# State updates of a retention layer in column tiles, one chunk's v on another DMA queue, and three chunks' attention one tile later

## The chip, the cores and the metric

The kernel runs on one core of one Trainium2 chip. The metric is the device time of one execution in microseconds (us); lower is better. Five executions of the kernel before gave 211.85 to 213.12 us, with a median of 212.31 us. One of these executions (212.75 us) was taken with the hardware profiler, and all views of the kernel before are of that one.

## What is computed

The first half is a retention layer (linear attention with a decay for each head), the second a two-layer network with a gelu between its layers, without biases. Cut to what matters:

```python
batch, n_heads, seq, head_dim = (4, 8, 768, 64)     # q, k, v
gamma = 1.0 - 2.0 ** (-5.0 - np.arange(H))
for t in range(S):
    state = gamma * state + einsum('bhd,bhe->bhde', k[:, :, t], v[:, :, t])
    y[:, :, t] = (1 / sqrt(D)) * einsum('bhd,bhde->bhe', q[:, :, t], state)
x = y.transpose(0, 2, 1, 3).reshape(B * S, H * D)   # 3072 tokens of 512
h = x @ w_in                                        # 512 x 2048
out = gelu_tanh(h) @ w_out                          # 2048 x 512
```

All inputs and the output are float32 in HBM; the kernel computes its matmuls in float16 with float32 sums.

## The kernel before

**Chunks.** The 768 steps of the sequence are cut into 6 chunks of 128 (c = 0 to 5). One chunk holds 128 steps of all 4 batches, 512 tokens. A chunk goes through attention first (all 8 heads, handled as 4 pairs, `hp` for the pair and `j` for the head in it) and then through the network. While the network of one chunk runs on TensorE, the attention of the next is mixed in.

**Attention of a chunk and batch.** k and q are scaled by powers of the decay. A is k times q transposed (`mm_A`), and is masked on VectorE (`ev_A`, tile a_sb). y is the sum of the old state times q (`mm_yc`, tile st, not in chunk 0) and of v times A (`mm_yi`); `ev_Y` casts it into xT, on ScalarE or VectorE. S is k times v, summed over the steps of the chunk; `ev_S` or `ev_S2` adds it to the decayed state stg and writes st; `decay` (GpSimd) makes the next stg from st. S has two forms in the kernel before. In chunks 0 and 1, `mm_s` multiplies a pair of heads at once, 4 matmuls of 128 columns for a batch, of which `ev_S` reads the two diagonal blocks. In chunks 2 to 4, `att_S2` makes one matmul of 64 columns for each head, 8 for a batch, in column tiles (two heads of a pair write the two halves of the PSUM partitions), the same tiling in which `mm_yi` makes y. Chunk 5 needs no S.

**Transposes.** For chunks 0 and 1, q and k are transposed on TensorE (`mm_T`, `mm_T1`). From chunk 2 on, they are loaded a second way, in blocks of 32 (`load_blk`: 16 transfers of 64 KB for q, tile q, and 16 for k, tile kT), scaled by `prep_blk` on GpSimd (L206) and transposed on VectorE (`tr`, L263). k itself is loaded too (`load1`, L98), since S needs it untransposed.

**Network.** `moe1` makes h_ps for one sixteenth of the 2048 columns of w_in (4 matmuls of 512 columns) and `gelu` (ScalarE) writes g. `moe2` makes a quarter of o_ps of one batch (4 matmuls of 512 columns), and `ev_O` copies the finished o_ps to o_sb and issues its store, on GpSimd for most chunks. A unit below is one call of either, in chunks 2 to 5: 16 of `moe1`, then 16 of `moe2`, four for each batch.

**Order.** The order of the work on each engine is the order in which the program writes it; no scheduler moves anything. `run(units, after)` writes the units one after the other, and behind unit i the calls listed in `after[i]`. That is where the attention of the next chunk sits among the matmuls of this one. On its engine each instruction waits for what it needs, and all behind it wait too. PSUM has 8 banks, of which `bank` hands out 2 under the tag h, 2 under o and 4 under att, in turn, so that a tile waits for the one that had its bank before.

**Loads.** SyncE issues most loads, one after another, in program order: the rest of chunk 1, then q and kT blocks of chunk 2, then three outputs of chunk 0 kept back in `late`, then k of chunk 2, then all of chunk 3 (`load(3)`). In the built program each transfer of SyncE or ScalarE also waits for a semaphore last used by the one issued eight earlier. v of chunks 0, 1 and 3 to 5 is loaded as float32 and cast (on ScalarE, VectorE or GpSimd, `prep1`). v of chunk 2 alone comes through `load_v16`: GpSimd issues four transfers that convert to float16 on the way, with no cast behind them. GpSimd's list around it is:

```python
            7: [(prep, 2, "Q"), (load_v16, 2)],
            8: [(tr, 2, "q")],
            10: [(prep, 2, "Kk")],
```

Capital letters in `prep` stand for the block form (`prep_blk`), small ones for `prep1`. The first loads of chunk 1 on SyncE are held back with a dummy copy (`hold`, L124) until the third part of w_out has landed.

Of the kernel before, what the change touches and what calls it, by code (L numbers as in the profile page):

```python
# [16 lines left out]
def kernel(  # L17
# [11 lines left out]
    C = 128  # L29
# [67 lines left out]
    def load1(eng, nm, c, b):  # L97
        eng.dma_start(  # L98
            out=ld_tile(nm, c, b),
            in_=srcs[nm][b, :, c * C:(c + 1) * C, :].rearrange("h p d -> p h d"),  # L100
        )
# [81 lines left out]
    def prep1(eng, nm, c, b):  # L183
        t = pre.tile(
            [128, H, Dh], F16, tag=f"{nm}16", bufs=6 if nm == "q" else 2 * B, name=f"{nm}16"
        )
        src = ld_tile(nm, c, b)
        if nm == "v":
            if eng is nc.scalar:
                eng.copy(out=t, in_=src)  # L190
            else:
                eng.tensor_copy(out=t, in_=src)
        else:
            col = OQ if nm == "q" else OK
            eng.tensor_tensor(  # L195
                out=t,
                in0=src,
                in1=cst[:, col:col + H].unsqueeze(2).broadcast_to([128, H, Dh]),
                op=ALU.mult,
            )  # L200
        h16[nm, c, b] = t
# [12 lines left out]
    def pair(t, hp):  # L214
        return t[:, 2 * hp:2 * hp + 2]
# [6 lines left out]
    def copy_on(eng, out, in_):  # L222
        if eng is nc.scalar:
            eng.copy(out=out, in_=in_)  # L224
        else:
            eng.tensor_copy(out=out, in_=in_)  # L226
# [5 lines left out]
    def bank(tag, dt=F32, shape=(128, NHP, 128), name="ps"):  # L232
        return psum.tile(list(shape), dt, tag=tag, bufs=BANKS[tag], name=name)
# [70 lines left out]
    def mm_yi(c, b):  # L304
        y_ps = pss["Y", c, b]
        for hp in range(NHP):
            for j in range(2):
                nc.tensor.matmul(  # L308
                    out=y_ps[j * 64:(j + 1) * 64, hp],
                    lhsT=h16["v", c, b][:, 2 * hp + j],  # L310
                    rhs=a_sb[c, b, j][:, hp],
                    start=(c == 0),
                    stop=True,
                    skip_group_check=True,
                )

    def ev_Y(c, b, eng=nc.vector):
        if c not in xT:
            xT[c] = xp.tile([128, NHP, B * C], F16, tag="x", name="xT")
        copy_on(eng, xT[c][:, :, b * C:(b + 1) * C], pss.pop(("Y", c, b)))  # L320

    def mm_s(c, b, tag="att"):
        if c + 1 >= NCk:
            return
        s_ps = pss["S", c, b] = bank(tag, name="s_ps")
        for hp in range(NHP):
            nc.tensor.matmul(  # L327
                out=s_ps[:, hp],
                lhsT=pair(h16["k", c, b], hp),
                rhs=pair(h16["v", c, b], hp),  # L330
                start=True,
                stop=True,
            )

    def ev_S(c, b, eng=nc.vector):
        if c + 1 >= NCk:
            return
        s_ps = pss.pop(("S", c, b))
        for j in range(2):
            sl = slice(j * 64, (j + 1) * 64)  # L340
            if c == 0:
                copy_on(eng, st[sl, :, b, sl], s_ps[sl, :, sl])
            else:
                eng.tensor_tensor(  # L344
                    out=st[sl, :, b, sl],
                    in0=s_ps[sl, :, sl],
                    in1=stg[sl, :, b, sl],
                    op=ALU.add,
                )

    def decay(c, b):
        if c + 2 < NCk:
            nc.gpsimd.tensor_tensor(  # L353
                out=stg[:, :, b],
                in0=st[:, :, b],
                in1=cst[:, OG:OG + NHP].unsqueeze(2).broadcast_to([128, NHP, 128]),
                op=ALU.mult,
            )
# [3 lines left out]
            mm_T(c, b)  # L362
            ev_T(c, b)

    def att_S2(c):

        if c + 1 >= NCk:
            return
        for b in range(0, B, 2):
            s_ps = bank("att", shape=(128, 2, NHP, 64), name="s_ps")  # L370
            for i in range(2):
                for hp in range(NHP):
                    for j in range(2):
                        nc.tensor.matmul(  # L374
                            out=s_ps[j * 64:(j + 1) * 64, i, hp],
                            lhsT=h16["k", c, b + i][:, 2 * hp + j],
                            rhs=h16["v", c, b + i][:, 2 * hp + j],
                            start=True,
                            stop=True,
                            skip_group_check=True,  # L380
                        )
            pss["S2", c, b] = s_ps

    def ev_S2(c, b):
        if c + 1 >= NCk:
            return
        s_ps = pss["S2", c, b // 2 * 2]
        for j in range(2):
            sl = slice(j * 64, (j + 1) * 64)
            nc.vector.tensor_tensor(  # L390
                out=st[sl, :, b, sl],
                in0=s_ps[sl, b % 2],
                in1=stg[sl, :, b, sl],
                op=ALU.add,
            )
        decay(c, b)

    def att_S(c, b, tag="att"):
        mm_s(c, b, tag)
        ev_S(c, b)  # L400
        decay(c, b)

    def att_Y(c):

        tags = ("h", "h", "att", "att")
        for b in range(B):
            mm_yc(c, b, tags[b])
        for b in range(B):
            mm_yi(c, b)
        att_S2(c)  # L410
        for b in range(B):
            ev_Y(c, b, (AC, VE)[b % 2])

    def att_AY(c, bs, tag, ca, abs_, eng):


        for b in bs:
            mm_yc(c, b, tag)
        for b in abs_:
            mm_A(ca, b)  # L420
        for b in bs:
            mm_yi(c, b)
        if tag == "o":
            for b in abs_:
                ev_A(ca, b)
        for b in bs:
            ev_Y(c, b, eng)
        if tag != "o":
            for b in abs_:
                ev_A(ca, b)  # L430
# [184 lines left out]
    ev_T1("q", 0, 3, AC)  # L615
    spin(4)
    mm_A(0, 3)
    mm_s(0, 0)
    mm_yc(0, 2, "o")
    mm_yi(0, 2)  # L620
    prep1(AC, "v", 0, 3)
    ev_Y(0, 2, AC)
    ev_A(0, 3)
# [3 lines left out]
    m1a = [moe1_parts(0, fp, *t01) for fp in range(2)]  # L627
    m1a[0](range(2))
    m1a[1](range(2))
    mm_s(0, 1)  # L630
    mm_yc(0, 3, "o")
    mm_yi(0, 3)
    ev_Y(0, 3)
    mm_s(0, 2)
    mm_s(0, 3)
    m1a[0](range(2, 4))
    m1a[1](range(2, 4))
    for b in range(2):
        moe1_two(0, b, *t23, "oh"[b])
    for b in range(B):  # L640
        ev_S(0, b)
        decay(0, b)


    hold("q", 1, 1, w_out_sb[2][0:1, 0, 0:1])
# [23 lines left out]
    for nm, b in (  # L669
# [9 lines left out]
            11: [(load1, AC, "v", 1, 2), (prep1, AC, "v", 1, 0), (att_AY, 1, (), "att", 1, (0,), None)],  # L679
            12: [(prep1, AC, "v", 1, 1), (att_T, 1, 1), (preps, 1, 2)],  # L680
            13: [(att_AY, 1, (0,), "h", 1, (1,), AC)],
            14: [(prep1, AC, "v", 1, 2), (att_T, 1, 2), (preps, 1, 3), (att_S, 1, 0)],
            15: [
                (att_AY, 1, (1,), "h", 1, (2,), AC),
                (att_T, 1, 3),
                (att_S, 1, 1),
            ],
        },
    )
# [3 lines left out]
    load_blk("k", 2)  # L693
    for rows, o_sb in late:
        nc.sync.dma_start(out=rows, in_=o_sb)
    for b in range(B):
        load1(SY, "k", 2, b)
    load(3)

    def load_v16(c):  # L700

        for b in range(B):
            t = pre.tile([128, H, Dh], F16, tag="v16", bufs=2 * B, name="v16")
            nc.gpsimd.dma_start(
                out=t, in_=v[b, :, c * C:(c + 1) * C, :].rearrange("h p d -> p h d")
            )
            h16["v", c, b] = t

    def prep(c, nms):

        for nm in nms:
# [9 lines left out]
        {  # L721
            0: [(prep1, AC, "v", 1, 3)],
            1: [(att_AY, 1, (2,), "o", 1, (3,), VE)],
            3: [(att_S, 1, 2)],
            4: [(att_AY, 1, (3,), "o", 1, (), VE)],
            6: [(att_S, 1, 3)],
            7: [(prep, 2, "Q"), (load_v16, 2)],
            8: [(tr, 2, "q")],
            10: [(prep, 2, "Kk")],
        },  # L730
    )
    run(
# [2 lines left out]
            1: [(tr, 2, "k", 0, 1)],  # L735
            3: [(att_AY, 2, (), "att", 2, (0, 1), None), (tr, 2, "k", 2, 3)],
            7: [(att_AY, 2, (), "att", 2, (2, 3), None)],
            11: [(att_Y, 2)],
            12: [(ev_S2, 2, 0)],
            13: [(ev_S2, 2, 1)],  # L740
            14: [(ev_S2, 2, 2)],
            15: [(ev_S2, 2, 3)],
        },
    )

# [1 line left out]
    for c in range(2, NCk - 1):  # L747
        n = c + 1
        after = {
            2: [(prep, n, "QKvk"), (tr, n, "q")],  # L750
            9: [(load, n + 1)] if n + 1 < NCk else [],
            15: [(tr, n, "k", 0, 1)],
            18: [(att_AY, n, (), "att", n, (0, 1), None), (tr, n, "k", 2, 3)],
            22: [(att_AY, n, (), "att", n, (2, 3), None)],
            26: [(att_Y, n)],
            27: [(ev_S2, n, 0)],
            28: [(ev_S2, n, 1)],
            29: [(ev_S2, n, 2)],
            30: [(ev_S2, n, 3)],
        }  # L760
        run(
            [(lambda fc=fc: moe1(c, fc)) for fc in range(NF)]
            + [x for b in range(B) for x in units2(c, b)],
            after,
        )
# [37 lines left out]
```

## Time and profile before

| | value |
|---|---|
| median of 5 executions | 212.31 us (211.85 to 213.12) |
| the profiled execution | 212.75 us, span 210.7 us (first to last instruction) |
| granted TensorE clock | full, in all 40 slices |
| busy: TensorE, GpSimd, VectorE, ScalarE | 203.9, 102.0, 92.3, 83.6 us |
| o_ps matmuls of 512 columns (L513) | 368, one each 0.216 us when back to back |
| h_ps matmuls of 512 columns (L468) | 304, likewise |
| SyncE's queue (q1) | 20.22 MB, 50.1% of 16 engines' span |
| GpSimd's queue (q0) | 9.44 MB, 21.9% |

A line of the timeline gives the start and the length of a group of like instructions in us, the engine, the source line, the output and inputs, the shape and the count, and in brackets how long the engine had been idle before it and which instruction ended that. PE is TensorE's matmul stream, DVE VectorE, ACT ScalarE, POOL GpSimd, SPq the DMA issues of SyncE. The chain of work is followed back from the last instruction to what released it, step by step; a line gives start, length and what it was. The 0.216 us above is 13.81 us of the chain for 64 h_ps matmuls.

### The profile page before, as it was taken

The numbers are of one execution on the slowest core, as the hardware profiler recorded it, in microseconds if no ns is written. First come the engines' busy times: TensorE is split into PE (matmuls) and PEld (weight loads), VectorE is DVE, ScalarE is ACT, GpSimd is POOL, SyncE is SP. The second block draws the span as 40 slices with busy tenths as digits, with TensorE's granted clock in tenths as the row PEclk, the third lists the DMA queues.
The fourth block names the chain that finished last, engine by engine and source line by source line (L and its number), as shares of the span: only waits on it lengthen the run. The fifth ranks groups of instructions, "written<-read, shape, count | busy, mean of one in ns | idle before, by whom it ended". The sixth has DMA issues, their size and how long they took to land.

```text
span 210.7 us, 3948 instructions
## 1 busy us (share of the span) xinstructions
PE 203.9 (97%) x1550; PEld 109.5 (52%) x1550; DVE 92.3 (44%) x163; ACT 83.6 (40%) x142; POOL 102.0 (48%) x123
## 2 busy tenths in 40 slices
PE   7999999999999699999999999999999999999993
PEld 2458444467886246444446444456444455444452
DVE  5797100399542675450767352567460552100001
ACT  2375660246464113366113466113466113565120
POOL 3589300317278756862892959731598411100100
PEclk9999999999999999999999999999999999999999
DMA  7999999998879997979979899897996021100112
GB/s 160 288 237 169 206 202 199 272 237 171 130 110 125 241 188 183 215 121 186 270 123 200 174 203 238 158 199 121 206 252 136 0 101 53 50 0 0 53 54 97
DMA packets 132691, 33.32 MB, mean 158 GB/s; under 512 B 126528, under 2 KB 130880, under 8 KB 132672
## 3 DMA queue, kind: packets, MB, share of 16 engines
q1 hardware_dynamic: 111088, 20.22, 50.1%
q0 software_dynamic: 9856, 9.44, 21.9%
q10 hardware_dynamic: 11728, 3.41, 7.1%
q8 instruction: 12, 0.20, 0.4%
q14 instruction: 7, 0.06, 0.1%
HBM read 31.48 MB, written 6.29 MB: 179 GB/s over the span
## 4 chain that ended last, share of the span: by engine, by line
PE 83%; SPq 8%; DVE 3%; DMA 2%; issue 2%; POOL 1%; DVEq 0%
PE o_ps L513 37%; PE h_ps L468 33%; SPq L110 8%; PE spin_ps L171 3%; PE a_ps L273 2%; PE y_ps L308 2%; DMA kT<-in_k_dram 2%; PE y_ps L295 2%; DVE q L195 1%; POOL kT L206 1%; PE s_ps L374 1%; DVE a_sb L286 1%; PE qkT_ps L239 1%; PE qkT_ps L252 1%; PE s_ps L327 1%
## 5 line engine op out<-in xcount | busy, mean ns | idle before, releaser
L513 PE MATMUL o_ps<-w_out,g 128*128 128x512 f16 (+1 forms) x400 | 86.9, 371 | 0.0
L468 PE MATMUL h_ps<-xT,w_in 128*128 128x512 f16 (+1 forms) x464 | 85.1, 342 | 0.0
L483 ACT ACTIVATE g<-h_ps 128x512 f16<-128x512 f32 x96 | 56.9, 597 | 44.8 <-PE h_ps L468 44.7
L468 PEld LDWEIGHTS <-w_in 128*128 128x128 f16 x464 | 45.0, 98 | 37.7 <-issue 0.3
L513 PEld LDWEIGHTS <-g 128*128 128x128 f16 x400 | 37.9, 98 | 41.1 <-issue 0.2
L286 DVE TENSOR_TENSOR a_sb<-a_ps,mask 128x512 f16<-128x512 f32 x48 | 30.1, 682 | 17.2 <-PE a_ps L273 17.0
L535 ACT COPY o_sb<-o_ps 128x512 f32<-128x512 f32 x19 | 11.1, 586 | 53.8 <-PE o_ps L513 51.0
L195 POOL TENSOR_TENSOR k<-k,cst 128x512 f16<-128x512 f32 x23 | 23.9, 1061 | 16.1 <-DMA k<-in_k_dram 16.1
L540 POOL DMA_DIRECT2D out_dram<-o_sb x18 | 10.1, 562 | 44.6 <-ACT o_sb L535 34.7
L206 POOL TENSOR_TENSOR kT<-kT,cst 128x512 f16<-128x512 f32 x16 | 16.2, 1042 | 8.8 <-DMA kT<-in_k_dram 6.5
L353 POOL TENSOR_TENSOR stg<-st,cst 128x512 f32<-128x512 f16 x16 | 16.3, 1055 | 7.5 <-DVE st L344 3.8
L263 DVE STREAM_TRANSPOSE qkT<-kT 128x512 f16<-128x512 f16 x16 | 10.9, 697 | 14.8 <-POOL kT L206 14.8
L263 DVE STREAM_TRANSPOSE qkT<-q 128x512 f16<-128x512 f16 x16 | 11.4, 712 | 13.4 <-POOL q L206 13.4
L206 POOL TENSOR_TENSOR q<-q,cst 128x512 f16<-128x512 f32 x16 | 16.2, 1046 | 0.5 <-DMA kT<-in_k_dram 0.4
L195 DVE TENSOR_TENSOR q<-q,cst 128x512 f16<-128x512 f32 x8 | 7.0, 870 | 16.5 <-DMA q<-in_q_dram 16.5
L226 DVE CAST xT<-y_ps 128x512 f16<-128x512 f32 x11 | 7.2, 686 | 12.9 <-PE y_ps L308 12.9
L551 DVE COPY o_sb<-o_ps 128x256 f32<-128x256 f32 x2 | 0.8, 424 | 26.6 <-PE o_ps L513 26.6
L224 ACT CAST xT<-y_ps 128x512 f16<-128x512 f32 x13 | 7.2, 587 | 11.2 <-PE y_ps L308 11.0
L171 PE MATMUL spin_ps<-zero 128*128 128x512 f16 x30 | 10.1, 477 | 1.3 <-DVE zero L139 1.3
L390 DVE TENSOR_TENSOR st<-s_ps,stg 64x256 f16<-64x256 f32 x24 | 10.1, 421 | 0.7
L273 PE MATMUL a_ps<-qkT 64*128 64x128 f16 x192 | 8.3, 218 | 2.1 <-DVE qkT L263 1.8
L273 PEld LDWEIGHTS <-qkT 64*128 64x128 f16 x192 | 5.4, 94 | 7.6 <-DVE qkT L263 2.9
(43 smaller groups left out, 92.7 us busy)
## 6 DMA issues: line engine op xcount, KB each, us to landing
k<-in_k_dram SPq DMA_DIRECT2D x20, 256.0 KB, 4.4
out_dram<-o_sb POOLq DMA_DIRECT2D x18, 256.0 KB, 2.9
v<-in_v_dram SPq DMA_DIRECT2D x17, 256.0 KB, 4.4
q<-in_q_dram SPq DMA_DIRECT2D x64, 64.0 KB, 2.9
kT<-in_k_dram SPq DMA_DIRECT2D x64, 64.0 KB, 2.8
w_out<-in_moe_w_out_dram POOLq DMA_DIRECT2D x4, 512.0 KB, 16.3
q<-in_q_dram ACTq DMA_DIRECT2D x4, 256.0 KB, 8.8
k<-in_k_dram ACTq DMA_DIRECT2D x4, 256.0 KB, 8.6
```

The costliest lines, as they stand in the source:

```text
L110: nc.sync.dma_start(out=t[p0:p0 + 32, :, a, :], in_=src[j, dd, t0:t0 + 32])
L171: nc.tensor.matmul(out=ps, lhsT=zero[:, 0:128], rhs=zero, start=True, stop=True)
L195: eng.tensor_tensor(out=t, in0=src, in1=cst[:, col:col + H].unsqueeze(2).broadcast_to([128, H, Dh]), op=ALU.mult,)
L206: nc.gpsimd.tensor_tensor(out=t, in0=ld_all((key, c))[:, b * NHP:(b + 1) * NHP].rearrange("p hp a d -> p (hp a) d"), in1=cst[:, col:col + ...
L263: nc.vector.transpose(out=qkT_tile(c, b)[:, "qk".index(nm)].rearrange("p hp t -> p (hp t)"), in_=blk16.pop((nm, c, b)).rearrange("p ha d - ...
L273: nc.tensor.matmul(out=ps[j][:, hp], lhsT=t[j * 64:(j + 1) * 64, 1, hp], rhs=t[j * 64:(j + 1) * 64, 0, hp], start=True, stop=True,)
L286: nc.vector.tensor_tensor(out=s, in0=ps[j], in1=mask[:, j], op=ALU.mult)
L353: nc.gpsimd.tensor_tensor(out=stg[:, :, b], in0=st[:, :, b], in1=cst[:, OG:OG + NHP].unsqueeze(2).broadcast_to([128, NHP, 128]), op=ALU.mult,)
L468: nc.tensor.matmul(out=out, lhsT=w_in_of(fc, kc), rhs=xT[c][:, kc, t0:t1], start=(kc == 0 and first), stop=(kc == NHP - 1), skip_group_che ...
L483: nc.scalar.activation(out=out, in_=in_, func=AF.Gelu_apprx_tanh, scale=1.0)
L513: nc.tensor.matmul(out=ps[:, n0:n1], lhsT=g_sb[c, fc // 2][:, fc % 2, b * C:(b + 1) * C], rhs=w_out_sb[fc // (NF // NO)][:, fc % (NF // NO ...
L535: nc.scalar.copy(out=o_sb, in_=ps)
```

## The change

Three things change. First, `mm_s`, `att_S2`, `ev_S2` and `att_S` go; one `mm_S` makes S for one or two batches in the form of `att_S2`, and it is called straight behind `mm_yi` everywhere: in `att_Y`, in `att_AY` (so that S of chunk 1 moves ahead of where `att_S` stood) and, for two batches at a time, in chunk 0. `ev_S` reads the dense tile and ends with `decay`; its places in the lists are those of `att_S`. Second, `load_v16` goes; v of chunk 2 is loaded by SyncE as float32, four transfers between the late outputs and k of chunk 2, and GpSimd casts it between kT and k ("Kvk"). Third, `att_Y` of chunk 2 goes from behind unit 11 to behind unit 12, ahead of `ev_S` of batch 0; for chunks 3 to 5, the k transposes, A, y and state updates all stand one unit later.

```diff
-    def mm_s(c, b, tag="att"):
+    def mm_S(c, bs, tag="att"):
         if c + 1 >= NCk:
             return
-        s_ps = pss["S", c, b] = bank(tag, name="s_ps")
-        for hp in range(NHP):
-            nc.tensor.matmul(out=s_ps[:, hp], lhsT=pair(h16["k", c, b], hp),
-                             rhs=pair(h16["v", c, b], hp), start=True, stop=True)
+        s_ps = bank(tag, shape=(128, 2, NHP, 64), name="s_ps")
+        for i, b in enumerate(bs):
+            for hp in range(NHP):
+                for j in range(2):
+                    nc.tensor.matmul(out=s_ps[j * 64:(j + 1) * 64, i, hp],
+                                     lhsT=h16["k", c, b][:, 2 * hp + j],
+                                     rhs=h16["v", c, b][:, 2 * hp + j],
+                                     start=True, stop=True, skip_group_check=True)
+            pss["S", c, b] = s_ps[:, i]
...
@@ ev_S
-                copy_on(eng, st[sl, :, b, sl], s_ps[sl, :, sl])
+                nc.vector.tensor_copy(out=st[sl, :, b, sl], in_=s_ps[sl])
...
+        decay(c, b)
@@ att_Y
-        att_S2(c)
+        for b in range(0, B, 2):
+            mm_S(c, (b, b + 1))
@@ att_AY
         for b in bs:
             mm_yi(c, b)
+            mm_S(c, (b,))
@@ chunk 0
     mm_A(0, 3)
-    mm_s(0, 0)
     mm_yc(0, 2, "o")
     mm_yi(0, 2)
+    mm_S(0, (0, 1))
...
-    mm_s(0, 1)
     mm_yc(0, 3, "o")
     mm_yi(0, 3)
+    mm_S(0, (2, 3))
     ev_Y(0, 3)
-    mm_s(0, 2)
-    mm_s(0, 3)
@@ chunk 1, in the lists
-            (att_S, 1, b)
+            (ev_S, 1, b)
@@ loads of chunk 2
-    for b in range(B):
-        load1(SY, "k", 2, b)
+    for nm in "vk":
+        for b in range(B):
+            load1(SY, nm, 2, b)
     load(3)
@@ during the network of chunk 1
-            7: [(prep, 2, "Q"), (load_v16, 2)],
+            7: [(prep, 2, "Q")],
             8: [(tr, 2, "q")],
-            10: [(prep, 2, "Kk")],
+            10: [(prep, 2, "Kvk")],
...
-            11: [(att_Y, 2)],
-            12: [(ev_S2, 2, 0)],
+            12: [(att_Y, 2), (ev_S, 2, 0)],
@@ during the network of chunks 2 to 4 (n = 3 to 5)
-            15: [(tr, n, "k", 0, 1)],
-            18: [(att_AY, n, (), "att", n, (0, 1), None), (tr, n, "k", 2, 3)],
-            22: [(att_AY, n, (), "att", n, (2, 3), None)],
-            26: [(att_Y, n)],
-            27: [(ev_S2, n, 0)],
+            16: [(tr, n, "k", 0, 1)],
+            19: [(att_AY, n, (), "att", n, (0, 1), None), (tr, n, "k", 2, 3)],
+            23: [(att_AY, n, (), "att", n, (2, 3), None)],
+            27: [(att_Y, n)],
+            28: [(ev_S, n, 0)],
...
```

More of the change, by code (lines that the diff above doesn't have):

```diff
@@ L320, in ev_Y, with ev_S @@
         copy_on(eng, xT[c][:, :, b * C:(b + 1) * C], pss.pop(("Y", c, b)))
-    def mm_s(c, b, tag="att"):
+    def mm_S(c, bs, tag="att"):
         if c + 1 >= NCk:
             return
-        s_ps = pss["S", c, b] = bank(tag, name="s_ps")
-        for hp in range(NHP):
[L327 to L335, printed above, removed]
+        s_ps = bank(tag, shape=(128, 2, NHP, 64), name="s_ps")
+        for i, b in enumerate(bs):
+            for hp in range(NHP):
+                for j in range(2):
+                    nc.tensor.matmul(
+                        out=s_ps[j * 64:(j + 1) * 64, i, hp],
+                        lhsT=h16["k", c, b][:, 2 * hp + j],
+                        rhs=h16["v", c, b][:, 2 * hp + j],
+                        start=True,
+                        stop=True,
+                        skip_group_check=True,
+                    )
+            pss["S", c, b] = s_ps[:, i]
+    def ev_S(c, b):
         if c + 1 >= NCk:
@@ L341, in ev_S @@
             if c == 0:
-                copy_on(eng, st[sl, :, b, sl], s_ps[sl, :, sl])
+                nc.vector.tensor_copy(out=st[sl, :, b, sl], in_=s_ps[sl])
             else:
[L344 to L348, printed above, removed]
+                nc.vector.tensor_tensor(
+                    out=st[sl, :, b, sl], in0=s_ps[sl], in1=stg[sl, :, b, sl], op=ALU.add
                 )
+        decay(c, b)
     def decay(c, b):
@@ L363, in att_T @@
             ev_T(c, b)
[L365 to L401, printed above, removed]
     def att_Y(c):
@@ L641 @@
         ev_S(0, b)
-        decay(0, b)
     hold("q", 1, 1, w_out_sb[2][0:1, 0, 0:1])
@@ L681 @@
             13: [(att_AY, 1, (0,), "h", 1, (1,), AC)],
-            14: [(prep1, AC, "v", 1, 2), (att_T, 1, 2), (preps, 1, 3), (att_S, 1, 0)],
+            14: [(prep1, AC, "v", 1, 2), (att_T, 1, 2), (preps, 1, 3), (ev_S, 1, 0)],
             15: [
@@ L685 @@
                 (att_T, 1, 3),
-                (att_S, 1, 1),
+                (ev_S, 1, 1),
             ],
@@ L695 @@
         nc.sync.dma_start(out=rows, in_=o_sb)
-    for b in range(B):
-        load1(SY, "k", 2, b)
+    for nm in "vk":
+        for b in range(B):
+            load1(SY, nm, 2, b)
     load(3)
[L700 to L707, printed above, removed]
     def prep(c, nms):
@@ L723 @@
             1: [(att_AY, 1, (2,), "o", 1, (3,), VE)],
-            3: [(att_S, 1, 2)],
+            3: [(ev_S, 1, 2)],
             4: [(att_AY, 1, (3,), "o", 1, (), VE)],
-            6: [(att_S, 1, 3)],
-            7: [(prep, 2, "Q"), (load_v16, 2)],
+            6: [(ev_S, 1, 3)],
+            7: [(prep, 2, "Q")],
             8: [(tr, 2, "q")],
-            10: [(prep, 2, "Kk")],
+            10: [(prep, 2, "Kvk")],
         },
@@ L737 @@
             7: [(att_AY, 2, (), "att", 2, (2, 3), None)],
-            11: [(att_Y, 2)],
-            12: [(ev_S2, 2, 0)],
-            13: [(ev_S2, 2, 1)],
-            14: [(ev_S2, 2, 2)],
-            15: [(ev_S2, 2, 3)],
+            12: [(att_Y, 2), (ev_S, 2, 0)],
+            13: [(ev_S, 2, 1)],
+            14: [(ev_S, 2, 2)],
+            15: [(ev_S, 2, 3)],
         },
@@ L751 @@
             9: [(load, n + 1)] if n + 1 < NCk else [],
-            15: [(tr, n, "k", 0, 1)],
-            18: [(att_AY, n, (), "att", n, (0, 1), None), (tr, n, "k", 2, 3)],
-            22: [(att_AY, n, (), "att", n, (2, 3), None)],
-            26: [(att_Y, n)],
-            27: [(ev_S2, n, 0)],
-            28: [(ev_S2, n, 1)],
-            29: [(ev_S2, n, 2)],
-            30: [(ev_S2, n, 3)],
+            16: [(tr, n, "k", 0, 1)],
[3 more added lines that the diff above has]
+            28: [(ev_S, n, 0)],
+            29: [(ev_S, n, 1)],
+            30: [(ev_S, n, 2)],
+            31: [(ev_S, n, 3)],
         }
```

## The prediction

> **What bounds the kernel now.** I read the page first, then the chain of work that ended last, then TensorE's timeline for its gaps, then the timelines of GpSimd and SyncE around the one gap of size.
>
> ```profile
> span 210.7 us, 3948 instructions
> ...
> PE 203.9 (97%) x1550; PEld 109.5 (52%) x1550; DVE 92.3 (44%) x163; ACT 83.6 (40%) x142; POOL 102.0 (48%) x123
> ...
> PE 83%; SPq 8%; DVE 3%; DMA 2%; issue 2%; POOL 1%; DVEq 0%
> ```
>
> TensorE has work nearly all the time, yet the chain leaves it for SyncE's queue (SPq, 8%). That is where a cut can pay. In order of time the chain reads there:
>
> ```profile
> 64.29 0.49 SPq L110
> 64.82 3.98 DMA kT<-in_k_dram
> 68.80 0.07 issue
> 68.87 2.06 POOL kT L206 x2
> 70.96 0.72 DVE qkT L263
> 71.68 0.05 issue
> 71.73 0.40 PE a_ps L273 x8
> ```
>
> The last of the 32 block loads of chunk 2 starts at 64.82, lands at 68.80, GpSimd scales two batches, VectorE transposes them, and only then can TensorE begin A of chunk 2. TensorE's timeline shows the price, and how S runs in both forms:
>
> ```profile
> 17.40 0.62 PE L327 MATMUL s_ps<-v,k 128*128 128x128 f16 x8
> ...
> 65.88 3.62 PE L513 MATMUL o_ps<-w_out,g 128*128 128x512 f16 x16
> 70.72 0.40 PE L273 MATMUL a_ps<-qkT 64*128 64x128 f16 x8 [1.22 <-DVE qkT L263]
> 71.73 0.40 PE L273 MATMUL a_ps<-qkT 64*128 64x128 f16 x8 [0.61 <-DVE qkT L263]
> ...
> 80.62 1.08 PE L308 MATMUL y_ps<-a_sb,v 128*64 128x128 f16 x32
> 81.54 0.67 PE L374 MATMUL s_ps<-v,k 128*64 128x64 f16 x32
> ```
>
> 1.22 + 0.61 = 1.83 us idle at 69.5 to 71.7. After it the timeline shows no other gap up to the end: the last 139 us are TensorE alone. GpSimd, in the same stretch:
>
> ```profile
> 64.25 3.57 POOL L704 DMA_DIRECT2D v<-in_v_dram  x4
> 68.87 4.06 POOL L206 TENSOR_TENSOR kT<-kT,cst 128x512 f16<-128x512 f32 x4 [1.05 <-DMA kT<-in_k_dram]
> 75.83 3.05 POOL L195 TENSOR_TENSOR k<-k,cst 128x512 f16<-128x512 f32 x3 [2.90 <-DMA k<-in_k_dram]
> 79.94 1.04 POOL L195 TENSOR_TENSOR k<-k,cst 128x512 f16<-128x512 f32 x1 [1.05 <-DMA k<-in_k_dram]
> ```
>
> The four loads of v that the change removes begin at 64.25, just ahead of the last kT load, and k of chunk 2 is ready at 80.98, only 0.56 us before S at 81.54.
>
> **The change part by part.**
>
> *S of chunks 0 and 1 in column tiles.* Removed: 8 groups of 4 matmuls 128x128 (L327): in the chain 0.33, 0.22 and 0.55 us in chunk 0 (1.10) and about 0.22 for each of four batches in chunk 1 (0.90). Added: 8 groups of 8 matmuls 128x64 behind y. The nearest row is L374 in chunk 2, 32 in 0.50 us of the chain, 15.6 ns each, so 8 x 8 x 15.6 ns = 1.0 us. Saved on TensorE: 2.0 - 1.0 = 1.0 us. A rule of the Trainium skill speaks against this ("TensorEngine Tiling (Array Packing)", Instruction Overhead): a matmul of one column takes as long as one of 60, so splitting what is already small should not pay. From it I estimate 64 columns at full occupancy, 27 ns at the 2.4 GHz that its page "Trainium Kernel Development and Optimization", NeuronCore Architecture, gives: 64 x 27 ns = 1.7 us, a saving of 0.3. The row decides, since it is this very shape behind this very y.
>
> But I count almost none of that 1.0 us. In chunk 0, the first h_ps matmuls of the second half of w_in come at 17.85, and their weights (issued at 12.46, 5.2 us to landing) land at 17.66: at most 0.2 of the 0.6 us survives. The last part of w_out (issued 18.3, 20.5 us to landing) lands at 38.8, and its first use stands at 38.8: whatever survived waits there. In chunk 1, S of batch 1 now sits ahead of the transposes of batch 3 and takes the PSUM bank that ev_S of batch 0 frees at 49.16; y ends at 48.89, so TensorE waits 0.3 us there, and the transposes behind it need k of batch 3, ready on GpSimd only at 49.27: no loss, no gain. S of batches 2 and 3 give 0.1 each. So TensorE comes to A of chunk 2 at 69.1 to 69.3 instead of 69.4, and that is ahead of kT.
>
> *v of chunk 2.* Off GpSimd go four issues (3.57 us); on come four casts, 0.61 us each by the row of chunk 3's v (L192), placed after the four kT. GpSimd was waiting for kT anyway, so it loses nothing before kT. What matters is the DMA. The last kT load took 3.98 us where the one before took 2.6, and where chunk 3's last, with SyncE loads behind it but no v from GpSimd's queue, took 2.8. Here too a rule speaks against: "DMA: Bandwidth & Descriptors", Issuing engines are not separate DMA queues, says that all queues run on the same 16 engines, and that issuing from another saves only issue time. By it alone the bytes are the same and nothing is won. But the order is not the same: v now stands behind kT and the three late outputs in SyncE's queue rather than beside kT. I take 2.8 (chunk 3's row): kT lands at 67.6, 1.2 us sooner. Bounds: 2.3 (the shortest kT row) gives 1.7; still 3.98 gives 0. From a GpSimd start at 67.7, the measured 2.86 us to the second A puts it at 70.5 instead of 71.73. The gap falls to about 0.3 + 0.6 us, and TensorE's remaining work is unchanged: **gain 1.2 us**.
>
> *What v is moved past.* SyncE issues v x4 and then k x4, q x16, kT x16 and the eight v and k of chunk 3. If v and k flow as in chunk 3 (eight issues from 96.10 to 103.05, last landing 106.3) behind 0.79 MB of outputs, k of batch 3 lands at 78.5; at the 217 GB/s of the stretch 95 to 103, 2.88 MB from 67 on last until 80.3. Before, with the same transfers in two queues, it was 79.9. I take 79.5. v is in by 75 or 76, its casts end about 76.5, four k at 1.02 us each follow: done at 80.6. S of chunk 2 now starts one tile (4 x 0.216 us) later: 81.54 - 1.2 + 0.86 = 81.2, its last batch at 81.6. No stall, with about 1 us to spare; without that tile the spare would be 0.1.
>
> *One tile later, chunks 3 to 5.* No instruction is added. In chunk 3, A would be wanted at 102.11 - 1.2 + 0.86 = 101.8; its transposes are done at 100.4 and 101.4 as now, if SyncE's stream is where it was. The tile keeps the slack that the earlier TensorE would eat. At the other end y has 16 matmuls (3.5 us) before the next h_ps instead of 20. The casts of y ended 1.0 us after y: covered. ev_S of the last batch moves behind the o_sb copy on VectorE, and its decay behind one output issue on GpSimd: 1 to 2 us later, wanted a chunk later. Cost nil; if that cover were gone, 0.43 x 2 + 1.04 = 1.9 us. On a bound of below nothing: the A now stands between whole batches of o_ps instead of inside one, with equal counts of tile changes, so I see none.
>
> Sum against the profiled execution: 212.75 (span 210.7 and 2.05 around it) - 1.2 = 211.55. That execution is 0.44 above the median of 212.31, so against the median: **211.1**.
>
> **The rivals.**
>
> *No gain, kT still late.* If the outputs behind it, or chance, made the last kT late, it lands at 68.8 again and A starts at 71.7. For: one kT load of 16 is a thin base. Against: its neighbours at 2.6, and v starting in between. Time 212.2 (0.1 to 0.3 us from other edges).
>
> *SyncE's queue becomes the bound: slower.* The four k loads alone held SyncE from 67.14 to 75.68, 2.1 us each. If v takes as long without relieving k, all behind it moves by up to 8.5 us. kT of chunk 3 then decides: its second A has 0.6 us of slack, so a delay d costs d - 0.6; with the 1.2 gained it is slower beyond d = 1.8 us. At d = 4: +2.2 us, 214.5. S of chunk 2 would stall with it, but before it. Against: the 8.5 us include the sharing with v, the byte count is the same, and chunk 3's eight loads took 0.87 us each.
>
> *More gain.* ev_S of chunk 1 ends earlier, and if chunk 1's loads also come in earlier, SyncE's chain from 46.4 on starts earlier and kT lands by 67.2 or before: all 1.83 us of the gap go, and some of the 0.3 us of TensorE's lead: 210.3. For: ACT issues some of these loads after gelus. Against: SyncE waits until 35.56 for w_out, which is DMA.
>
> **How the numbers follow.** Main case 0.67 (211.1, its own range 210.6 to 211.7), no gain 0.12 (212.2), SyncE bound 0.13 (213 to 215), more gain 0.08 (210.3). A measurement here can tell about 0.5%, 1.06 us, from no change; the main case lies just beyond it, so two thirds of it (0.45) and all of the last (0.08) are faster, with some 0.02 of luck: 0.55. Same: 0.22 of the main case, the no-gain case, less that 0.02: 0.32. Slower 0.13. The range 210.3 to 212.8 leaves out most of the SyncE case and the far end of the last.
>
> **What would show it.** Right: last kT of chunk 2 at 2.4 to 3.0 us to landing; A of chunk 2 about 70.5 with under 1 us idle; GpSimd's k done before 81; no idle at s_ps, and A of chunk 3 without a wait; waits of some tenths at w_in (17.7) and at s_ps of chunk 1. Wrong: a kT of 4 us again; PE waiting at s_ps for k in chunk 2, or at a_ps in chunk 3 behind SyncE; a gap ahead of h_ps after y.

## The result, and the profile after

The changed kernel takes 210.97 us in the median of 40 runs (210.18 to 211.93), the kernel before 212.02 us in 77. The ratio is 0.9948, with a 95% interval of 0.9937 to 0.9960: 1.1 us faster. The prediction said 211.1, faster by 1.2. The profiled execution took 211.76 us against 212.75. Ratios leave out executions over 1.5% above the fastest of their kernel; the profile of "S alone" below is of such a one (215.37 us, granted clock 0.99).

The page of the changed kernel (busy time and instructions of each engine; the chain that ended last, by engine):

```profile
span 209.7 us, 4015 instructions
...
PE 202.5 (97%) x1582; PEld 109.0 (52%) x1582; DVE 91.6 (44%) x163; ACT 83.5 (40%) x142; POOL 101.3 (48%) x123
...
PE 75%; SPq 9%; DMA 9%; DVE 3%; POOL 1%; issue 1%; DVEq 0%
```

The chain still leaves TensorE for SyncE's queue with a like share, so that limit has not gone. It has moved. (The larger share of DMA lies at the start, in the first loads of k and w_in, ahead of 17.7 us.) The chain in order of time has SyncE one chunk later, at kT of chunk 3:

```profile
96.51 0.49 SPq L110
97.10 2.56 DMA v<-in_v_dram
99.66 2.05 POOL kT L206 x2
101.73 0.72 DVE qkT L263
102.50 0.40 PE a_ps L273 x8
```

(The DMA line names v, which was in flight then; the last kT load, issued at 96.51, landed 2.8 us later, at 99.3, and GpSimd's instruction begins at 99.66.) TensorE's timeline has every wait from chunk 0's network on, with what ended it in brackets:

```profile
17.73 13.31 PE L435 MATMUL h_ps<-xT,w_in 128*128 128x256 f16 x72 [0.69 <-DMA w_in<-in_moe_w_in_dram]
...
48.49 0.29 PE L330 MATMUL s_ps<-v,k 128*64 128x64 f16 x8
49.83 0.38 PE L239 MATMUL qkT_ps<-iden,q 128*128 128x128 f16 x4 [1.05 <-DVE st L349]
...
66.17 3.62 PE L480 MATMUL o_ps<-w_out,g 128*128 128x512 f16 x16
69.72 0.62 PE L273 MATMUL a_ps<-qkT 64*128 64x128 f16 x16
...
80.62 0.67 PE L330 MATMUL s_ps<-v,k 128*64 128x64 f16 x32
...
101.49 0.40 PE L273 MATMUL a_ps<-qkT 64*128 64x128 f16 x8 [0.24 <-DVE qkT L263]
102.50 0.40 PE L273 MATMUL a_ps<-qkT 64*128 64x128 f16 x8 [0.61 <-DVE qkT L263]
```

The 1.83 us at A of chunk 2 are gone: its 16 matmuls start at 69.72 without a wait. Three waits are new: 0.69 at w_in, 1.05 at a transpose of chunk 1, 0.85 at A of chunk 3. The account along TensorE: the first h_ps of chunk 2 stands at 83.82 instead of 85.61, a gain of 1.79 us; the first h_ps of chunk 3 at 116.38 instead of 117.07, a gain of 0.69. So chunk 3 took back 1.1: the 0.85 of waiting, and 0.25 for an A that runs in two halves. The last o_sb copy is 0.69 earlier too (206.67 against 207.36), and some 0.3 us of the span differ behind it, in the last store.

GpSimd in the same stretch:

```profile
66.76 4.07 POOL L206 TENSOR_TENSOR kT<-kT,cst 128x512 f16<-128x512 f32 x4 [3.42 <-DMA kT<-in_k_dram]
...
74.60 0.61 POOL L192 CAST v<-v 128x512 f16<-128x512 f32 x1 [0.22 <-DMA v<-in_v_dram]
75.51 1.04 POOL L195 TENSOR_TENSOR k<-k,cst 128x512 f16<-128x512 f32 x1 [0.30 <-DMA k<-in_k_dram]
77.18 3.06 POOL L195 TENSOR_TENSOR k<-k,cst 128x512 f16<-128x512 f32 x3 [0.62 <-DMA k<-in_k_dram]
...
99.64 4.07 POOL L206 TENSOR_TENSOR kT<-kT,cst 128x512 f16<-128x512 f32 x4 [4.75 <-DMA v<-in_v_dram]
```

kT of chunk 2 starts 2.1 us sooner (68.87 before); kT of chunk 3 starts 1.1 later (98.58 before). k of chunk 2 ends at 80.24, just ahead of S at 80.62.

### The profile page after: what moved, and what is told of

It is laid out like the page before. It is cut to its first block, busy times and chain, and to the rows that moved or that the text cites. A ratio compares the mean times of both kernels' runs of the same rounds, so it can differ in the third digit from the quotient of the medians.

```text
span 209.7 us, 4015 instructions
## 1 busy us (share of the span) xinstructions
PE 202.5 (97%) x1582; PEld 109.0 (52%) x1582; DVE 91.6 (44%) x163; ACT 83.5 (40%) x142; POOL 101.3 (48%) x123
## 3 DMA queue, kind: packets, MB, share of 16 engines
HBM read 31.48 MB, written 6.29 MB: 180 GB/s over the span
## 4 chain that ended last, share of the span: by engine, by line
PE 75%; SPq 9%; DMA 9%; DVE 3%; POOL 1%; issue 1%; DVEq 0%
PE o_ps L480 35%; PE h_ps L435 33%; SPq L110 9%; DMA k<-in_k_dram 5%; DMA w_in<-in_moe_w_in_dram 3%; PE a_ps L273 2%; PE y_ps L308 2%; PE y_ps L295 2%; DMA v<-in_v_dram 1%; POOL kT L206 1%; PE qkT_ps L239 1%; DVE a_sb L286 1%; PE s_ps L330 1%; DVE q L195 1%; POOL k L195 0%
## 5 line engine op out<-in xcount | busy, mean ns | idle before, releaser
L263 DVE STREAM_TRANSPOSE qkT<-kT 128x512 f16<-128x512 f16 x16 | 10.9, 698 | 17.7 <-POOL kT L206 17.7
L349 DVE TENSOR_TENSOR st<-s_ps,stg 64x256 f16<-64x256 f32 x32 | 13.4, 420 | 0.8
L195 DVE TENSOR_TENSOR q<-q,cst 128x512 f16<-128x512 f32 x8 | 6.3, 786 | 16.4 <-DMA q<-in_q_dram 16.4
L192 POOL CAST v<-v 128x512 f16<-128x512 f32 x16 | 9.6, 613 | 7.6 <-DMA v<-in_v_dram 7.6
```

Source lines behind the costliest of these rows:

```text
L195: eng.tensor_tensor(out=t, in0=src, in1=cst[:, col:col + H].unsqueeze(2).broadcast_to([128, H, Dh]), op=ALU.mult,)
L263: nc.vector.transpose(out=qkT_tile(c, b)[:, "qk".index(nm)].rearrange("p hp t -> p (hp t)"), in_=blk16.pop((nm, c, b)).rearrange("p ha d - ...
L349: nc.vector.tensor_tensor(out=st[sl, :, b, sl], in0=s_ps[sl], in1=stg[sl, :, b, sl], op=ALU.add)
```

## The experiments

Theory T: the gain is v's move alone, through kT of chunk 2; the shorter S is waited away; the later tile keeps the gain at A of chunk 3. Rivals: the gain is the shorter S (S); the move alone does it with no debt later (V). Ratios are to the kernel before, run beside each kernel on the same chip. The first four kernels share one chip, as do the next four and the last four.

**v alone.**

```diff
-    for b in range(B):
-        load1(SY, "k", 2, b)
+    for nm in "vk":
+        for b in range(B):
+            load1(SY, nm, 2, b)
...
-            7: [(prep, 2, "Q"), (load_v16, 2)],
+            7: [(prep, 2, "Q")],
-            10: [(prep, 2, "Kk")],
+            10: [(prep, 2, "Kvk")],
```

> The kernel before with one part of the change: v of chunk 2 over SyncE's queue with four casts on GpSimd, S and the lists as before. Theory T (the gain is kT of chunk 2 landing sooner once v is out of GpSimd's queue, and the tile's delay keeps it): last kT load 2.3 to 2.9 us to landing, the wait at the second A of chunk 2 mostly gone (under 0.7 us in all instead of 1.83), but A of chunk 3 is wanted 1.2 to 1.8 us sooner without the tile and waits for SyncE's stream there 1.2 to 2 us: total within 0.4 us of before. Theory V (v's move alone is the gain): 1.0 us faster than before. Theory S (the gain is TensorE's shorter S): no change at all, and the wait at A of chunk 2 as before.

Measured: 0.9979 (0.9954 to 1.0004), 212.04 us. Its TensorE timeline, waits only:

```profile
69.78 0.40 PE L273 MATMUL a_ps<-qkT 64*128 64x128 f16 x8 [0.30 <-DVE qkT L263]
...
100.82 0.40 PE L273 MATMUL a_ps<-qkT 64*128 64x128 f16 x8 [0.48 <-DVE qkT L263]
101.83 0.40 PE L273 MATMUL a_ps<-qkT 64*128 64x128 f16 x8 [0.61 <-DVE qkT L263]
```

The second A of chunk 2 starts at 69.78 instead of 71.73, and 1.09 us of that are waited at A of chunk 3 (1.2 to 2 expected), where the kernel before had no wait. That is theory T's picture. Note the interval: by itself, v's move is not shown to make the kernel faster.

**S alone.** The changed kernel with `load_v16` back and the lists of before:

```diff
+            7: [(prep, 2, "Q"), (load_v16, 2)],
+            10: [(prep, 2, "Kk")],
+            11: [(att_Y, 2)],
...
+            15: [(tr, n, "k", 0, 1)],
+            18: [(att_AY, n, (), "att", n, (0, 1), None), (tr, n, "k", 2, 3)],
+            22: [(att_AY, n, (), "att", n, (2, 3), None)],
+            26: [(att_Y, n)],
```

> The kernel before with another part alone: S of all chunks in column tiles behind y; v of chunk 2 through GpSimd's queue and the lists one tile earlier, as before. Theory T: TensorE's saving is waited away at w_in (0.5 to 0.7 us at 17.7), at the transposes of chunk 1's batch 3 (about 1 us) and at A of chunk 2 behind kT: within 0.3 us of before. Theory S: 0.7 to 1.1 us faster than before.

Measured: 1.0031 (0.9994 to 1.0068). No gain; theory S falls. Its profile shows v on GpSimd's queue once more: the last four kT loads of chunk 2 took 3.4 to 5.0 us to landing, and TensorE waited at A of chunk 2.

**No tile.** The changed kernel with the lists of before (11; 15, 18, 22, 26 and on).

> The changed kernel with the lists of before (attention of chunks 2 to 5 one tile sooner). Theory T: A of chunk 3 is set by SyncE's stream and starts where it did (second A at about 102.5), with one unit of o_ps more behind it (0.86 us): 0.7 to 1.0 us slower than the changed kernel, that is 0.1 to 0.4 us faster than before; the waits at A of chunk 3 sum to 1.7 us or more. Theory V or S (the tile does nothing): as the changed kernel, 1.1 us faster than before.

Measured: 0.9952 (0.9934 to 0.9970), 211.04 us: as the changed kernel, where theory T wanted 0.7 to 1.0 slower. Its only wait after chunk 1 is at S of chunk 3:

```profile
111.41 0.32 PE L330 MATMUL s_ps<-v,k 128*64 128x64 f16 x8 [0.42 <-POOL k L195]
```

kT of chunk 3 was ready to be scaled at 97.78 in this execution, 1.9 us sooner than in the changed kernel's profile. So the start of A of chunk 3 is not anchored where I had put it, and the tile is not shown to be what keeps the gain. This kernel is the one with v alone plus the new S, on the same chip (211.04 us against 212.04); the intervals of the two ratios overlap, so whether S helps where the tile is absent stays open.

**Chunk 3 a further tile later.**

```diff
-            16: [(tr, n, "k", 0, 1)],
-            19: [(att_AY, n, (), "att", n, (0, 1), None), (tr, n, "k", 2, 3)],
-            23: [(att_AY, n, (), "att", n, (2, 3), None)],
-            27: [(att_Y, n)],
+            16 + x: [(tr, n, "k", 0, 1)],          # x is 1 for n == 3, else 0
+            19 + x: [(att_AY, n, (), "att", n, (0, 1), None), (tr, n, "k", 2, 3)],
+            23 + x: [(att_AY, n, (), "att", n, (2, 3), None)],
+            27 + x: [(att_Y, n)],
```

> The changed kernel with the attention of chunk 3 alone one further tile later (its y then has 12 matmuls behind it instead of 16). Theory T: the wait of 0.85 us at A of chunk 3 and the 0.25 us of the tile change between its two halves go, nothing else opens: 0.8 to 1.1 us faster than the changed kernel, ratio to before 0.989 to 0.991. Rival (the next limit is at the same place, SyncE's stream for v and k of chunk 3 or the casts of y before h_ps of chunk 3): at most 0.3 us faster than the changed kernel, with a new wait at s_ps or h_ps of chunk 3.

Measured: 0.9933 (0.9910 to 0.9956), 210.64 us, with a span of 208.3 and no wait on TensorE from 50 us on. It lies between theory and rival: its interval overlaps that of the kernel without the tile. kT of chunk 3 started at 97.42, so there was little to wait for in any case.

**No v of chunk 2.** The four transfers are left out, and with them GpSimd's time to issue them; chunk 2 uses v of chunk 1, so the output is not the layer's.

```diff
-            nc.gpsimd.dma_start(out=t, in_=v[b, :, c * C:(c + 1) * C, :].rearrange("h p d -> p h d"))
-            h16["v", c, b] = t
+            h16["v", c, b] = h16["v", c - 1, b]
```

> The kernel before without any load of v of chunk 2; chunk 2 uses v of chunk 1 in its place, so four transfers are left out. Theory T (v on GpSimd's queue delays the last kT): last kT load 2.3 to 2.9 us to landing instead of 4.0, wait at A of chunk 2 under 0.9 us; k of chunk 2 and all of chunk 3 come in 2 to 4 us sooner than before, so A of chunk 3 does not wait: 1.2 to 1.8 us faster than before, ratio 0.992 to 0.994. Rival (the outputs behind kT in SyncE's own queue delay it): last kT about 4 us, wait at A of chunk 2 as before, within 0.3 us of before.

Measured: 0.9940 (0.9912 to 0.9968). The last kT of chunk 2 landed in 2.4 us, the outputs behind it as ever, and TensorE waits neither at A of chunk 2 nor of chunk 3. GpSimd's timeline:

```profile
66.94 4.07 POOL L206 TENSOR_TENSOR kT<-kT,cst 128x512 f16<-128x512 f32 x4 [1.80 <-DMA kT<-in_k_dram]
...
93.43 4.07 POOL L206 TENSOR_TENSOR kT<-kT,cst 128x512 f16<-128x512 f32 x4 [2.00 <-DMA kT<-in_k_dram]
```

kT of chunk 3 is here at 93.4, 5.2 us sooner than in the kernel before and four to six sooner than in the kernels that load v through SyncE. The outputs fall as the cause; and it is v's load, on either queue, that takes the room in SyncE's stream. The gain is no larger than the changed kernel's, since TensorE came to A of chunk 2 only at 70.26.

**v and the tile, the old S.** The kernel with v alone, plus the changed lists.

> v over SyncE's queue and the lists one tile later, but S as before (pairs in chunks 0 and 1, at the old places): the changed kernel without its S part. Theory T (S gives nothing): as the changed kernel or up to 0.4 us faster, ratio to before 0.993 to 0.996, since the transposes of chunk 1's batch 3 do not wait for a bank (0.7 to 1.05 us in the runs with the new S). Rival (S is needed for the gain, by what it leaves to chunks 2 and 3): as the run with v alone, ratio 0.997 to 0.999.

Measured: 0.9936 (0.9907 to 0.9965). The changed kernel without its S part is as fast as with it. One wait is left from chunk 1 on:

```profile
70.22 0.40 PE L273 MATMUL a_ps<-qkT 64*128 64x128 f16 x8 [0.61 <-DVE qkT L263]
```

At A of chunk 3 nothing, with kT of chunk 3 started at 98.71; the run with v alone had it at 98.97 and waited 1.09. This pair has the tile's sign as predicted, though the two intervals overlap.

**S of chunk 1 at its old places.**

```diff
         for b in bs:
             mm_yi(c, b)
-            mm_S(c, (b,))
...
+    def att_S(c, b):
+        mm_S(c, (b,))
+        ev_S(c, b)
-            (ev_S, 1, b)
+            (att_S, 1, b)
```

> The changed kernel with S of chunk 1 in column tiles but issued at its old places, just ahead of ev_S. Theory T: no wait at the transposes of chunk 1's batch 3; TensorE comes to A of chunk 2 0.3 to 0.5 us sooner and waits there for kT 0.1 to 0.4 us, or at A of chunk 3: within 0.4 us of the changed kernel. Rival (that wait is on the path that sets the end): 0.6 to 1.0 us faster than the changed kernel.

Measured: 0.9907 (0.9871 to 0.9943), 210.67 us in six runs that agree within 0.2. The wait at chunk 1's transposes is gone and no A waits, but TensorE comes to A of chunk 2 at 69.69, as in the changed kernel (69.72). Its median is 0.3 us below the changed kernel's.

**Both.** That, and the further tile for chunk 3.

> The last kernel's S of chunk 1 at its old places together with chunk 3's attention one further tile later. Theory T: with the room at A of chunk 3, what TensorE gains in chunk 1 is kept up to the wait for kT at A of chunk 2: 0.1 to 0.4 us faster than the further tile alone, ratio to before 0.9915 to 0.993. Rival (the wait moves in full): as the further tile alone, 0.993 to 0.994.

Measured: 0.9912 (0.9881 to 0.9944), 210.77 us: nothing on top of the last one. The room at A of chunk 3 was not needed (kT at 98.29, no wait there; 0.21 us at A of chunk 2).

**The tile alone.** The kernel before with the changed lists.

> The third part of the change alone: the kernel before with y of chunk 2 and all attention of chunks 3 to 5 one tile later. Theory T: the 1.83 us of waiting at A of chunk 2 stands, chunk 3 had no wait to lose: within 0.3 us of before. Rival (the later tile itself shortens or lengthens a stage, for example the casts of y with less behind them): over 0.5 us either way, seen as a wait at h_ps or s_ps.

Measured: 1.0004 (0.9983 to 1.0026). The tile by itself is nothing, as predicted. Its profile shows a second price of v on GpSimd's queue. GpSimd's timeline, then TensorE's:

```profile
63.92 3.57 POOL L704 DMA_DIRECT2D v<-in_v_dram  x4
67.47 4.09 POOL L206 TENSOR_TENSOR kT<-kT,cst 128x512 f16<-128x512 f32 x4
```

```profile
69.36 0.40 PE L273 MATMUL a_ps<-qkT 64*128 64x128 f16 x8 [0.19 <-DVE qkT L263]
70.37 0.40 PE L273 MATMUL a_ps<-qkT 64*128 64x128 f16 x8 [0.61 <-DVE qkT L263]
```

In this execution the last kT (issued 63.7) landed in 2.5 us, at 66.2. But GpSimd was still issuing v, until 67.49, and began kT at once (no wait in brackets). TensorE waited 0.80 us rather than 1.83. This execution took 211.37 us, the shortest of its kernel.

**A of chunk 2 a tile later**, once with v, tile and old S, once with S of chunk 1 at its old places:

```diff
-            1: [(tr, 2, "k", 0, 1)],
-            3: [(att_AY, 2, (), "att", 2, (0, 1), None), (tr, 2, "k", 2, 3)],
-            7: [(att_AY, 2, (), "att", 2, (2, 3), None)],
+            2: [(tr, 2, "k", 0, 1)],
+            4: [(att_AY, 2, (), "att", 2, (0, 1), None), (tr, 2, "k", 2, 3)],
+            8: [(att_AY, 2, (), "att", 2, (2, 3), None)],
```

> v over SyncE's queue and the later lists with the old S, and chunk 2's k transposes and A one tile later too. Theory T: the 0.6 us of waiting at A of chunk 2 that the run with v and tile still had goes: 0.3 to 0.6 us faster than that run, ratio to before 0.991 to 0.993. Rival (the end is set by chunk 1 or SyncE's stream, and A of chunk 2 only shows it): same as that run, 0.9936.

> The changed kernel with S of chunk 1 at its old places, and chunk 2's k transposes and A one tile later. Theory T: no wait on TensorE from chunk 1 on in any execution: as the run with S at its old places or up to 0.3 us faster, ratio to before 0.989 to 0.992, and 0.3 to 0.7 us faster than the changed kernel beside it.

Measured: 0.9937 (0.9912 to 0.9962) and 0.9943 (0.9919 to 0.9967). No wait at any A, and neither is shown to be faster than the kernel it came from (0.9936 and 0.9907, on another chip). For the first that fits the rival, that the wait only showed a limit ahead of it; its interval also holds part of the 0.991 to 0.993 of theory T, so this is not settled.

**The changed kernel again**, beside the last three.

> The changed kernel itself, beside these three on one chip and with a second profile. Theory T: ratio to before 0.994 to 0.996; the wait for a bank at chunk 1's transposes is there again (0.7 to 1.1 us); the wait at A of chunk 3 comes and goes with SyncE's stream: with kT of chunk 3 ready to scale by 98 it is nil, at 99.6 it was 0.85 us. Rival (the wait at A of chunk 3 belongs to the change): 0.8 us or more again.

Measured: 0.9940 (0.9919 to 0.9960). TensorE's waits from chunk 1 on in its second profile:

```profile
49.31 0.38 PE L239 MATMUL qkT_ps<-iden,q 128*128 128x128 f16 x4 [0.35 <-DVE st L349]
70.35 0.40 PE L273 MATMUL a_ps<-qkT 64*128 64x128 f16 x8 [0.45 <-DVE qkT L263]
```

The wait at A of chunk 3 is absent (kT at 98.00) and 0.45 us at A of chunk 2 are there. So these waits belong to the execution, not to the kernel. The wait at the transposes is 0.35, below the 0.7 to 1.1 expected. The version with S at its old places and the later A is 0.9943 on this chip: none of these versions is shown to beat the changed kernel.

## Why the prediction was right, and where it was not

**The place and the mover were right.** The 1.83 us behind kT of chunk 2 were the thing to win, and v's move won them. Of fourteen profiles, the eleven without v on GpSimd's queue have the last kT load at 2.4 to 2.6 us, and GpSimd starts kT between 66.57 and 67.49. S alone and the tile alone give nothing; every kernel with v's move and one of the other two parts is 0.5 to 0.9% faster. v alone is not shown to be faster (0.9979, up to 1.0004).

**Why v delayed kT, in one execution and not in another.** The prediction put it down to v "starting in between" the last two kT loads. The order of issue does not bear that out: GpSimd began to issue v at 64.25, ahead of both (64.29 and 64.82), and the first of the two took 2.6 us. What counts is when v's packets move, which is 1.7 to 2.3 us after GpSimd begins to issue them. All three profiles with v on GpSimd's queue fit:

| profile | v's first packets | last kT issued, landed | time |
|---|---|---|---|
| kernel before | 66.00 | 64.82, 68.80 | 3.98 us |
| S alone (the slower execution) | 65.13 | 65.01, 69.98 | 4.98 us |
| tile alone | 66.20 | 63.70, 66.20 | 2.51 us |

With the tile alone, the last kT landed just as v began to move. In the kernel before it was still under way (the one ahead of it, which landed at 66.88, was not slowed). The DMA queues there from 66.0 to 67.5 (packets, MB, share of 16 engines; q0 is GpSimd's, q1 SyncE's), and with the tile alone from 64.0 to 66.2:

```profile
q0 software_dynamic: 539, 0.07, 71.0%
q1 hardware_dynamic: 268, 0.03, 22.6%
...
q1 hardware_dynamic: 1876, 0.44, 92.3%
```

The rule that the prediction set against itself, from the Trainium skill's page "DMA: Bandwidth & Descriptors" (Issuing engines are not separate DMA queues), is right that both queues run on the same 16 engines and interleave. That nothing but issue time is won by the choice of queue did not hold here: as many bytes were read (31.48 MB in both kernels), but v's came behind kT instead of beside it.

**One step beside it failed.** "GpSimd was waiting for kT anyway, so it loses nothing before kT" is true of the one profile that I had. The run with the tile alone shows the other case: kT landed in 2.5 us and then stood 1.3 us for GpSimd, which was still issuing v. With v gone from that queue both costs end. That may be why the step of 4.0 to 2.8 us, taken from one load, came out right for a median of executions that do not all have that tail; how often each case occurs was not measured.

**kT landed 0.9 us earlier than the sum.** I put it at 67.6; it landed at 66.7. The tail fell to 2.65 instead of 2.8, and the last kT was issued at 64.05 instead of 64.82. The dummy copy behind w_out, which lets SyncE's stream go, stood at 34.83 instead of 35.56 in this execution. Over the runs at full clock it lies at 34.83 to 35.46 with the new S and at 35.24 to 35.81 with the old; the ranges overlap, so I take most of this as spread.

**The cost of S ahead of chunk 1's transposes was mis-sized.** I wrote a wait of 0.3 us with "no loss, no gain". It was 1.05 in the profile, 0.35 (twice), 0.71 and 0.89 in the four others with the new S in that place, and it showed at the transposes, not at S. The prediction took the time at which `ev_S` frees the bank from the kernel before (49.16). On VectorE `ev_S` stands behind the scaling of q of batch 3, and that took 1.38 us in the changed kernel's first profile and 0.68 in its second. GpSimd's scaling of k and VectorE's of q, in the first profile, then VectorE's in the second:

```profile
47.39 1.04 POOL L195 TENSOR_TENSOR k<-k,cst 128x512 f16<-128x512 f32 x1 [2.90 <-DMA k<-in_k_dram]
47.61 1.38 DVE L195 TENSOR_TENSOR q<-q,cst 128x512 f16<-128x512 f32 x1
...
47.79 0.68 DVE L195 TENSOR_TENSOR q<-q,cst 128x512 f16<-128x512 f32 x1
```

In the second profile GpSimd began k only at 48.72. With 0.68 for q the wait is 0.35, about as predicted; in the five profiles it grows by what q takes beyond that. But this wait does not explain why TensorE came to A of chunk 2 at 69.72 rather than at 69.1 to 69.3: the run with S at its old places has no such wait and came at 69.69. Its ratio of 0.9907 hints at a gain, but its interval meets the changed kernel's.

**A of chunk 3: the rival was there in part.** I had kT of chunk 3 no later than before, and no wait. In the profile it came 1.1 us later and TensorE waited 0.85, by the mechanism of the SyncE rival (d = 1.1, beyond its slack of 0.6), short of the d = 1.8 from which it would decide. By the rival's formula, d - 0.6, it should have cost 0.5 and it cost 1.1, since TensorE, with more gained in chunk 2, came there at 101.25 instead of the 101.8 of the sum. In the second profile kT came at 98.00 and the wait was nil. Over the runs that load v through SyncE it lies at 97.4 to 99.6. The prediction had no spread for that term.

**Two sizes cancelled.** kT came sooner than the sum (gain 1.79 instead of 1.2 by chunk 2) and chunk 3 took 1.1 back, which leaves 0.69 on TensorE, and 1.0 in the time with the last store. The number 211.1 is right within 0.2 partly for that reason, and so far by luck.

**What went as written:** the 0.6 us saved in chunk 0 met w_in at 17.73 (0.69 waited there); k of chunk 2 was done at 80.24 (80.6 written) with no wait at S; the casts of y stayed covered. The prediction's estimate of 27 ns for a matmul of 64 columns, after the Trainium skill's page "TensorEngine Tiling (Array Packing)" (Instruction Overhead: one column takes as long as 60), was too high here: 8 take 0.12 us of the chain, 15 ns each, behind y, as the row had said.

**What stays open.** What sets TensorE's arrival at A of chunk 2 (69.1 to 70.3 over the runs) once nothing waits there: chunk 1's loads, behind w_out, are the candidate, and no run moved them. And whether the tile or S is worth anything beside v's move: v with and without the tile differ by 0.4%, the changed kernel with and without it by none; v with and without the new S differ by 0.3% in the old lists and by less than the noise in the new.

## What to carry to other kernels

A transfer issued by an engine that also computes can cost twice: its bytes share the DMA engines with what is on the critical path, and its issue (0.9 us each here) stands ahead of that engine's next work; ask for both, since one profile shows only the one that was last. The waits of under 2 us behind DMA differed here from one execution to the next by as much as the effect looked for (1.83 and 0.80 us, 0.85 and none), so give such a term a spread, and take a second profile before explaining it. Work taken off the bounding engine just ahead of waits for data was worth nothing here: 1 us of matmuls went and the time did not.

## What the runs showed of the hardware that was not expected

A 64 KB load at the end of SyncE's stream took 2.4 to 2.6 us in all ten profiles in which three outputs and the first load of v were issued behind it, on the same queue, before it landed. With v on GpSimd's queue it took 4.0 and 5.0 us where v's packets began to move before it had landed, and 2.5 us where they began as it landed. So transfers behind it on its own queue did not slow it, and transfers on another queue did, once they moved.

Where VectorE scales q and GpSimd scales k of batch 3 in chunk 1, the one that begins second takes longer, in all thirteen profiles in which the two overlap: q takes 0.68 us when it is first and 1.04 to 1.55 when it is second, k 1.04 when first and 1.16 to 1.45 when second. Each time k as the second ends 0.9 us after q, and q as the second 0.55 us after k, whatever the overlap, as if the second had waited for the first. No run was made to test this.
